# Packed attention with a gated feed-forward: pp @ w in groups of three f tiles, and where the attention's small products stand

## The chip, the cores and the metric

One core of one Trainium2 chip. The metric is the device time of one launch in microseconds (us); lower is better. Besides the times there is one profiled execution of the kernel, whose trace the rows below come from.

## What is computed

```python
def sm_attn(qq, kk, vv):
    s = scale * np.matmul(qq, kk.transpose(0, 1, 3, 2))
    ...                                  # softmax over the last axis -> a
    return np.matmul(a, vv)
p_packed = sm_attn(p, k, v)              # 8 batches, 8 heads, 32 packed rows
out = sm_attn(q, p_packed, p_packed)     # 576 rows a batch, 64 a head
...
x = out.transpose(0, 2, 1, 3).reshape(B * S, H * D)      # 4608 x 512
return ((x @ w_a) * (x @ w_b)) @ w_out   # w_a, w_b: 512 x 1536, w_out: 1536 x 512
```

All data are float32. The large products run as three products of parts (high by high, high by low, low by high), the small ones directly in float32.

## The kernel before

It works through eight batches. The second attention's last product and the two large products x @ w_a and x @ w_b are joined: out is a2 @ pp per head, so x @ w equals a2 times (pp @ w), and pp @ w (called g here) is small. For a batch, with the 1536 columns of w_a and w_b in twelve tiles of 128 (`ft` 0 to 11):

- **g** (`g_tiles`, matmuls on L332): eight products, of 64 rows by 32 columns each, for one pair of f tiles: four values of `r` by two of `e`, each with 512 moving columns (128 of w_a and 128 of w_b for both tiles). The four `r` stand on the four groups of 32 partitions of one PSUM bank, the two `e` in two banks of the pool `ps_x`. ACT casts each bank into `ghi` (L338), DVE subtracts for `glo` (L86).
- **mm1** (`mm1_half`, L351) for one f tile: 12 matmuls of 288 columns for w_a, then 12 for w_b, each half in a pair of banks of the pool `ps_m` ("m"), which has two such pairs that take turns. ACT copies the first half out (L363), DVE multiplies the second by it (L366), ACT casts the product to `h_hi` (L370), POOL makes `h_lo`.
- **mm2** (L377): after the twelve f tiles the batch's output tiles, each 36 matmuls of 512 columns; four or five such tiles a batch.

The order on each engine is written out by hand: instructions stand on their engine in the order in which the code calls them. Two things set it around the change. Pair c+1 of g is computed ahead of the odd tile `ft` = 2c+1 of the same batch; the first pair of the next batch is computed by the step `g` at the start of mm2. And the attention of the next batch is cut into steps, which the string `PLAN` deals out to numbered slots: `between` is called once after the first half and once after the second half of each mm1, and once after every three f tiles of mm2, so slots 2 ft and 2 ft + 1 belong to tile ft, and slots from 24 on to mm2. (`PLAN_0` does so for batch 0, which also has the weights to convert.) The steps that matter here:

- `S0`, `S1`: the first attention's scores for half e of the heads: 24 matmuls of 64 rows by 32 columns (each counts twice in a trace), L247, into the single pair of banks of the pool `ps_s` ("s").
- `r0`, `r1`, four times each: maximum and exponential; reciprocal; the transposes (L271 and L272, into "s"); the product with v (L281, 128 rows by 32 columns, into "s", then DVE L287 for `pp`).
- `T2 P0`: transposes of p and pp (L236). `s0`, `s1`: the second attention, begun by 16 recorded matmuls each on L297, e = 0 into "s" and e = 1 into "m"; DVE L302 then turns them.
- `q0`, `q1`, `k2`, `k3`: DVE turns a block of q or k (L119). `Lk`, `Lq`, `Lv`, `Lp`: SP issues loads.

In a trace each float32 matmul stands as two records, so a g of one pair is 16 records.

Of the kernel before, what the change touches and what calls it, by code (L numbers as in the profile page):

```python
# [9 lines left out]
F32R = mybir.dt.float32r  # L10
# [9 lines left out]
def tile_packed_attn_gated_ffn(  # L20
# [40 lines left out]
    ld = ep(tc.tile_pool(name="ld", bufs=1))  # L61
# [14 lines left out]
    w_ab = big.tile([P, NC, R, 4 * P], F32, name="w_ab")  # L76
# [154 lines left out]
    def turned(dst, src, back=0):  # L231

        tp = bank()
        cols = src.rearrange("p e d -> p (e d)")
        for i in range(2):
            nc.tensor.transpose(tp[:, P * i:P * i + P], cols[:, 64 * (i ^ back):64 * (i ^ back) + P], ident)  # L236
        nc.vector.tensor_copy(out=dst.rearrange("p i r j -> p (i r j)"), in_=tp[:, 0:2 * P])
# [84 lines left out]
        yield  # L322


    def g_tiles(b, c):

        assert len(to_do["C"]) <= len(pieces) - 4 * (c + 1)
        gps = [bank() for _ in range(E)]
        for r in range(R):
            for e in range(E):  # L330
                rows = slice(64 * e, 64 * e + 64)
                nc.tensor.matmul(  # L332
                    out=gps[e][J * r:J * r + J, :], lhsT=ppT[rows, 2 * (b % 2), r, :], rhs=w_ab[rows, c, r, :],
                    start=True, stop=True)
        ghi = ld.tile([P, E, 4 * P], F32R, name="ghi", bufs=2)
        glo = ld.tile([P, E, 4 * P], F32R, name="glo", bufs=2)
        for e in range(E):
            nc.scalar.copy(out=ghi[:, e], in_=gps[e])  # L338
            lo_part(glo[:, e], gps[e], ghi[:, e])
        gv = [t.rearrange("p e (a u f) -> p u e a f", a=2, u=2) for t in (ghi, glo)]  # L340
        return [(gv[0][:, u], gv[1][:, u]) for u in range(2)]


    def mm1_half(i, ghi, glo, ps=None, kts=range(E)):

        ps = bank_pair() if ps is None else ps
        steps = [(gt, at, kt) for kt in kts for gt, at in ((ghi, a2_hi), (ghi, a2_lo))]
        steps += [(glo, a2_hi, kt) for kt in kts]
        for n, (gt, at, kt) in enumerate(steps):
            for half in range(2):  # L350
                nc.tensor.matmul(  # L351
                    out=ps[:, half, 0:HS], lhsT=gt[:, kt, i, :], rhs=at[:, kt, HS * half:HS * half + HS],
                    start=(n == 0 and kt == 0), stop=(n == len(steps) - 1 and kt == E - 1))
        return ps

    def mm1(b, ft, ghi, glo, between):
        asb = sm.tile([P, 2, HS], F32, name="asb")
        if b == 0 and ft == 0:
            pa, pb = (mm1_half(i, ghi, glo, kts=(0,)) for i in range(2))
            mm1_half(0, ghi, glo, pa, (1,))  # L360
        else:
            pa, pb = mm1_half(0, ghi, glo), None
        nc.scalar.copy(out=asb, in_=pa[:, :, 0:HS])  # L363
        between()
        pb = mm1_half(1, ghi, glo, pb, (1,) if pb is not None else range(E))
        nc.vector.tensor_tensor(out=asb, in0=pb[:, :, 0:HS], in1=asb, op=ALU.mult)  # L366
        c0 = 64 * (b % 2)
        hh = h_hi[ft][:, c0:c0 + S]
        flat = asb.rearrange("p u t -> p (u t)")
        nc.scalar.copy(out=hh, in_=flat)  # L370
        lo_part(h_lo[ft][:, c0:c0 + S], flat, hh, nc.gpsimd)
        between()
# [43 lines left out]
    def drain(g):  # L416
        for _ in g:
            pass

    def emit(b, plan, tasks={}):  # L420

        for name in plan.split():
            if name in tasks:
                next(tasks[name], None)
                continue
            if name == "W":
                warm()
                continue
            if name in "ABCD":
                convert(name)  # L430
                continue
            what, e = name[:-1], int(name[-1])
            n = b + (e // 2 if b or what[0] == "L" else 0)
            if n >= B:
                continue
            if what == "S":
                if e == 0:
                    st[b] = [stage1(b, 0), stage1(b, 1), stage2(b, 0), stage2(b, 1)]
                next(st[b][e])
            elif what == "s":  # L440
                next(st[b][2 + e], None)
            elif what == "r":
                next(st[b][e], None)
            elif what == "T":
                turned(pT, p_nat.pop(n))
            elif what == "P":
                turned(ppT[:, b % 2:b % 2 + 2], pp.pop(b), b % 2)
            elif what in ("k", "q"):
                turn(what, n, e % 2) if b else turn_first(what, e)
            elif what == "Lk":  # L450
                load(k, "k", n, e % 2)
# [13 lines left out]
    TURN = ("0001110101")  # L465
    SUBS = ("0100")

    PLAN = (" | S0 | r0 |  | r0 | r0 |  | r0 Lv1 |  | S1 | r1 | q0 Lk2 | r1 |  |  | r1 q1 Lk3 |  | r1 Lv2 |  |  | "
            "T2 P0 |  |  | s0 s0 s1 g s0 |  | s1 | Lp4 s0 s1 s1 k2 | s0 | s0 | s1 s0 | s1 Lq2 | s1 | k3 Lq3")
    PLAN = dict(enumerate(PLAN.split("|")))  # L470
    PLAN_0 = ("A | C C | B A B A | B C C B C | A A | C | B | C B A T0 k0 Lp2 A | A A B B C Lq0 | C C k1 | A B A | "
# [5 lines left out]
    pieces = [(c, n) for c in range(NC) for n in range(4)] + [(NC, f) for f in range(NFT)]  # L477
    unloaded, to_do = list(pieces), {x: list(pieces) for x in "ABC"}
# [40 lines left out]
    def warm(n=9):  # L519

        x = bank_pair()[:, 0, :]
        t = firsts["k", 0].rearrange("p h t -> p (h t)")
        for _ in range(n):
            nc.tensor.matmul(out=x, lhsT=ident, rhs=t[:, 0:512], start=True, stop=True)

    def next_g(b):

        gnext[:] = g_tiles(b, 0)
        yield

    ET = mybir.EngineType
# [1 line left out]
    for name in FIRST.split():  # L533
        what, i = name[0], int(name[1])
# [5 lines left out]
            load_pieces(i)  # L540
        else:
            load_first(k if what == "k" else q, what, i)
    gnext = []
    tasks = {"g": next_g(0)}
    emit(0, START, tasks)
    drain(tasks["g"])
# [2 lines left out]
    for ft in range(NFT):  # L549
        h_hi.append(hp.tile([P, S + 64], F32R, name=f"h_hi{ft}"))  # L550
        h_lo.append(hp.tile([P, S + 64], F32R, name=f"h_lo{ft}"))

    for b in range(B):
        plan = dict(PLAN if b else PLAN_0)
        slot, tasks = [0], {"g": next_g(b + 1)}

        def between():
            emit(b + 1, plan.get(slot[0], "") if b + 1 < B else "", tasks)
            slot[0] += 1

        for ft in range(NFT):
            if ft % 2 == 0:
                gcur = list(gnext)
            elif ft + 1 < NFT:
                gnext[:] = g_tiles(b, ft // 2 + 1)
            mm1(b, ft, *gcur[ft % 2], between)
        tiles = [64 + P * i for i in range(4)] if b % 2 == 0 else [P * i for i in range(5)]
        last = tiles.pop() if b == B - 1 else None
        f0 = 0
        if b == 0:  # L570
            f0 = 9
            pairs = [bank_pair() for _ in range(2)]
            banks = [pairs[i % 2][:, i // 2, :] for i in range(4)]
            for f in range(f0):
                for i, c0 in enumerate(tiles):
                    mm2_part(banks[i], c0, [f])
                between()
            for _ in pieces:
# [50 lines left out]
```

## Time and profile before

| | us |
|---|---|
| median of 3 runs | 740.17 (739.3 to 740.57) |
| the profiled execution, its own time | 739.7 |
| its span, first to last instruction | 737.9 |
| TensorE (PE) busy | 724.8 |
| VectorE (DVE) busy | 302.4 |
| ScalarE (ACT) busy | 282.6 |
| GpSimd (POOL) busy | 212.5 |

The trace's views used below: the page's table of engines and its chain of waits by engine (which engine the end was waiting for, as shares of the span); the list of who waited for whom; the order of one engine's instructions in time, merged where alike; and busy times by stretch. A row of the order in time gives the start from the span's beginning in us, the time until its last record ends, engine, line, operation, output and inputs, shape, the count of records and, in brackets, how long the engine was idle before and for whom. Matmul records overlap, so the time that one takes from the next is the distance of their starts, not the length shown.

### The profile page before, as it was taken

Reading aid. Unit: us, or ns where it says so; the run is one execution under the profiler, and the core shown is the slowest. Engines: PE = TensorE matmul, PEld = TensorE weight load, DVE = VectorE, ACT = ScalarE, POOL = GpSimd, SP = SyncE. Lnnn points to the kernel's source line nnn. Section 1 sums busy time; section 2 is a strip of 40 time slices with the busy share of each in tenths; the row PEclk is TensorE's granted clock in tenths of the full one; section 3 lists DMA queues with packets and bytes.
Section 4 is the critical chain, followed back from the end, with each engine's and each line's share of the span. In section 5 each row is a group of like instructions: output and inputs, shape, how many; then the busy total and the mean of one; then the engine's idle time right before and its main releaser. Section 6 shows DMA issues by size and latency. Waiting matters only on the chain.

```text
span 737.9 us, 13756 instructions
## 1 busy us (share of the span) xinstructions
PE 724.8 (98%) x5862; PEld 606.0 (82%) x5862; DVE 302.4 (41%) x487; ACT 282.6 (38%) x495; POOL 212.5 (29%) x154
## 2 busy tenths in 40 slices
PE   6899999999999999999999999999999999999998
PEld 4488977888888888888888888888888888888887
DVE  2888655456114561344503545045610456023200
ACT  3788744553125531444204442144311543134300
POOL 0586752334003340234202341033400334023300
PEclk9999999999999999999999999999999999999999
DMA  8999945250501514033310333115050100000001
GB/s 251 379 260 297 257 88 99 57 97 17 97 30 33 98 30 84 16 66 70 74 48 16 65 71 77 47 33 97 5 104 30 34 1 17 28 15 2 1 29 43
DMA packets 171005, 58.30 MB, mean 79 GB/s; under 512 B 140608, under 2 KB 158784, under 8 KB 170944
## 3 DMA queue, kind: packets, MB, share of 16 engines
q1 hardware_dynamic: 170944, 57.43, 31.9%
q8 instruction: 46, 0.75, 0.4%
q14 instruction: 15, 0.12, 0.1%
HBM read 47.97 MB, written 9.44 MB: 78 GB/s over the span
## 4 chain that ended last, share of the span: by engine, by line
PE 95%; DVE 2%; DMA 1%; ACT 1%; issue 0%; SPq 0%; DVEq 0%; ACTq 0%
PE m L351 42%; PE m L377 40%; PE x L332 6%; PE s L281 2%; PE s L247 1%; PE s L271 1%; PE s L297 1%; DMA raw<-in_moe_w_b_dram 1%; DMA kn<-in_k_dram 1%; PE x L236 0%; DVE w_ab L200 0%; PE x L147 0%; PE m L297 0%; PE m L147 0%; SPq L177 0%
## 5 line engine op out<-in xcount | busy, mean ns | idle before, releaser
L377 PE MATMUL m<-wo,h_hi 128*128 128x512 f32 (+1 forms) x888 | 268.7, 385 | 0.0
L86 POOL TENSOR_TENSOR h_lo<-asb,h_hi 128x576 fp32r<-128x576 f32 x96 | 139.1, 1449 | 411.5 <-ACT h_hi L370 411.2
L377 PEld LDWEIGHTS m<-wo,h_hi 128*128 128x128 f32 x888 | 164.2, 188 | 39.0 <-DVE t L302 5.0
L366 DVE TENSOR_TENSOR asb<-m,asb 128x576 f32<-128x576 f32 x96 | 72.7, 757 | 281.9 <-PE m L351 278.6
L351 PE MATMUL m<-a_hi,ghi 128*128 128x288 f32 x768 | 170.7, 304 | 1.6 <-ACT ghi L338 1.5
L377 PE MATMUL m<-wo,h_lo 128*128 128x512 f32 (+1 forms) x444 | 170.4, 384 | 0.0
L351 PE MATMUL m<-a_lo,ghi 128*128 128x288 f32 x768 | 164.0, 295 | 0.3 <-DVE a_lo L86 0.3
L351 PEld LDWEIGHTS m<-a_hi,ghi 128*128 128x128 f32 x768 | 122.2, 188 | 37.5 <-issue 15.9
L351 PE MATMUL m<-a_hi,glo 128*128 128x288 f32 x768 | 133.5, 295 | 0.0
L351 PEld LDWEIGHTS m<-a_lo,ghi 128*128 128x128 f32 x768 | 123.5, 188 | 0.5 <-DVE a_lo L86 0.5
L370 ACT CAST h_hi<-asb 128x576 fp32r<-128x576 f32 x96 | 64.7, 674 | 143.6 <-DVE asb L366 143.5
L351 PEld LDWEIGHTS m<-a_hi,glo 128*128 128x128 f32 x768 | 112.8, 188 | 0.2 <-DVE glo L86 0.2
L377 PEld LDWEIGHTS m<-wo,h_lo 128*128 128x128 f32 x444 | 83.4, 188 | 16.6
L86 DVE TENSOR_TENSOR glo<-x,ghi 128x512 fp32r<-128x512 f32 x96 | 61.8, 686 | 53.3 <-ACT ghi L338 53.3
L363 ACT COPY asb<-m 128x576 f32<-128x576 f32 x96 | 61.6, 641 | 36.7 <-PE m L351 29.0
L412 ACT COPY asb<-m 128x512 f32<-128x512 f32 x24 | 14.1, 587 | 134.8 <-PE m L377 133.6
L332 PE MATMUL x<-w_ab,ppT 64*32 64x512 f32 x768 | 55.4, 597 | 0.2 <-DVE w_ab L200 0.2
L338 ACT CAST ghi<-x 128x512 fp32r<-128x512 f32 x96 | 51.4, 588 | 5.9 <-PE x L332 5.9
L119 DVE STREAM_TRANSPOSE xT<-nat 128x1152 f32<-128x1152 f32 x28 | 38.3, 1368 | 0.0
L412 ACT COPY wo_f<-m 128x512 f32<-128x512 f32 x11 | 6.5, 588 | 55.2 <-PE m L377 55.2
L315 POOL TENSOR_TENSOR t<-t,sum 128x576 f32<-128x576 f32 x14 | 16.5, 1178 | 25.0 <-DVE sum L314 25.0
L189 ACT ACTIVATE raw<-raw 128x512 f32<-128x512 f32 x36 | 23.1, 683 | 0.1
(108 smaller groups left out, 408.1 us busy)
## 6 DMA issues: line engine op xcount, KB each, us to landing
nat<-in_k_dram SPq DMA_DIRECT2D x56, 144.0 KB
nat<-in_q_dram SPq DMA_DIRECT2D x56, 144.0 KB
vt<-in_v_dram SPq DMA_DIRECT2D x28, 256.0 KB
raw<-in_moe_w_a_dram SPq DMA_DIRECT2D x12, 512.0 KB
raw<-in_moe_w_b_dram SPq DMA_DIRECT2D x12, 512.0 KB
raw<-in_moe_w_out_dram SPq DMA_DIRECT2D x12, 512.0 KB
out_dram<-asb SPq DMA_DIRECT2D x17, 256.0 KB
out_dram<-wo_f SPq DMA_DIRECT2D x10, 256.0 KB
```

What stands on the lines that cost most here:

```text
L86: return eng.tensor_tensor(out=dst, in0=src, in1=hi.bitcast(F32), op=ALU.subtract)
L119: nc.vector.transpose(out=xT.rearrange("p h t -> p (h t)"), in_=t.rearrange("p h x d -> p (h x d)"))
L189: nc.scalar.activation(out=high, in_=high, func=AF.Prelu, scale=2.0 ** -112, alpha=-2.0 ** 32)
L315: eng.tensor_tensor(out=s2, in0=s2, in1=sum2.unsqueeze(2).broadcast_to([P, TU, J]), op=ALU.mult)
L332: nc.tensor.matmul(out=gps[e][J * r:J * r + J, :], lhsT=ppT[rows, 2 * (b % 2), r, :], rhs=w_ab[rows, c, r, :], start=True, stop=True)
L338: nc.scalar.copy(out=ghi[:, e], in_=gps[e])
L351: nc.tensor.matmul(out=ps[:, half, 0:HS], lhsT=gt[:, kt, i, :], rhs=at[:, kt, HS * half:HS * half + HS], start=(n == 0 and kt == 0), stop= ...
L363: nc.scalar.copy(out=asb, in_=pa[:, :, 0:HS])
L366: nc.vector.tensor_tensor(out=asb, in0=pb[:, :, 0:HS], in1=asb, op=ALU.mult)
L370: nc.scalar.copy(out=hh, in_=flat)
L377: nc.tensor.matmul(out=o[:, cols], lhsT=ht[:, c0:c0 + P], rhs=wt[:, cols], start=(ft == 0 and n == 0), stop=(ft == NFT - 1 and n == 2))
L412: nc.scalar.copy(out=ob, in_=o)
```

## The change

In batches 1 to 7, g is computed for three f tiles at a time, four times a batch in place of six: ahead of tiles 2, 5 and 8, and at the step `g` in mm2. Each time one group has two tiles (512 columns, in two banks of `ps_x` as before) and one has a single tile (256 columns, the third). The third's two halves e stand in a pair of banks: the next of `ps_m` inside mm1 (issued ahead of the two-tile group), the pair of `ps_s` at the step in mm2 (issued behind it). `ghi` and `glo` become one tile each with four slots of an f tile; tile ft uses slot ft % 4. The number of columns is the same in all, as are the sizes in bytes of the casts and subtractions (128 x 512 for each). Batch 0 keeps its pairs. The columns of w are read in the order of f tiles, so the moving operand is read in runs of 128 columns.

`PLAN` is changed so that S0 stands in slot 3, and the product with v of r0 in slot 9, ahead of g; S1 comes in the same slot, behind g (a step after ";" is issued behind g). The product with v of r1 stands in slot 15, ahead of g. The transposes move from slots 5 and 15 to 7 and 13, `Lv1` from 7 to 9, `Lv2` from 17 to 15.

```diff
-    def g_tiles(b, c):
...
-        gps = [bank() for _ in range(E)]
-        for r in range(R):
-            for e in range(E):
-                rows = slice(64 * e, 64 * e + 64)
-                nc.tensor.matmul(
-                    out=gps[e][J * r:J * r + J, :], lhsT=ppT[rows, 2 * (b % 2), r, :], rhs=w_ab[rows, c, r, :],
-                    start=True, stop=True)
-        ghi = ld.tile([P, E, 4 * P], F32R, name="ghi", bufs=2)
-        glo = ld.tile([P, E, 4 * P], F32R, name="glo", bufs=2)
-        for e in range(E):
-            nc.scalar.copy(out=ghi[:, e], in_=gps[e])
-            lo_part(glo[:, e], gps[e], ghi[:, e])
...
+    ghi = ld.tile([P, E, 4, 2 * P], F32R, name="ghi")
+    glo = ld.tile([P, E, 4, 2 * P], F32R, name="glo")
+
+    def g_tiles(b, *groups, s=False):
+
+        for fts in groups:
+            c, i, n = fts[0] // 2, fts[0] % 4, len(fts)
...
+            if len(groups) > 1 and n == 1:
+                x = bank_pair(s)[:, :, 0:2 * P]
+                gps = [x[:, e, :] for e in range(E)]
+            else:
+                x, gps = None, [bank() for _ in range(E)]
+            for r in range(R):
+                for e in range(E):
+                    rows = slice(64 * e, 64 * e + 64)
+                    w = w_ab[rows, c, r, :].rearrange("p (a u f) -> p u a f", a=2, u=2)
+                    nc.tensor.matmul(
+                        out=gps[e][J * r:J * r + J, 0:2 * P * n], lhsT=ppT[rows, 2 * (b % 2), r, :],
+                        rhs=w if n == 2 else w[:, fts[0] % 2], start=True, stop=True)
+            parts = [(x, slice(0, E))] if x is not None else [(gps[e][:, 0:2 * P * n], e) for e in range(E)]
+            for part, e in parts:
+                hi, lo = (t[:, e, i] if n == 1 else t[:, e, i:i + 2].rearrange("p u c -> p (u c)") for t in (ghi, glo))
+                nc.scalar.copy(out=hi, in_=part)
+                lo_part(lo, part, hi)
...
-    PLAN = (" | S0 | r0 |  | r0 | r0 |  | r0 Lv1 |  | S1 | r1 | q0 Lk2 | r1 |  |  | r1 q1 Lk3 |  | r1 Lv2 |  |  | "
...
+    PLAN = (" |  |  | S0 | r0 | r0 |  | r0 |  | r0 Lv1 ; S1 | r1 | q0 Lk2 | r1 | r1 |  | r1 q1 Lk3 Lv2 |  |  |  | "
...
-        gnext[:] = g_tiles(b, 0)
+        g_tiles(b, *(((0, 1), (2,)) if b else ((0, 1),)), s=True)
...
+    G_AT = {2: ((3,), (4, 5)), 5: ((8,), (6, 7)), 8: ((9,), (10, 11))}
...
+            elif b and ft in G_AT:
+                g_tiles(b, *G_AT[ft])
+                emit(b + 1, late[0], tasks)
+            mm1(b, ft, between)
```

On TensorE, in a batch in the middle of the program. Before, the product with v of r0 (L281) stands by itself between two halves of mm1:

```order
L351 MATMUL m<-a_lo,ghi 128x288 x2
L351 MATMUL m<-a_hi,glo 128x288 x4
L281 MATMUL s<-vt,t_4232 32x64 x20
L351 MATMUL m<-a_hi,ghi 128x288 x2
L351 MATMUL m<-a_lo,ghi 128x288 x2
```

and one tile later the scores of S1 (L247) with a g of one pair (L332):

```order
L351 MATMUL m<-a_hi,glo 128x288 x4
L247 MATMUL s<-xT_3897,pT 32x288 x2
L247 MATMUL s<-xT_3985,pT 32x288 x2
L247 MATMUL s<-xT_3897,pT 32x256 x2
L247 MATMUL s<-xT_3985,pT 32x256 x2
L247 MATMUL s<-xT_3897,pT 32x32 x2
L247 MATMUL s<-xT_3985,pT 32x32 x2
L332 MATMUL x<-w_ab,ppT 32x512 x8
L351 MATMUL m<-a_hi,ghi 128x288 x2
```

Now, at the same place (lines have moved: g is L343, mm1 L361):

```order
L361 MATMUL m<-a_hi,glo 128x288 x4
L281 MATMUL s<-vt,t_4283 32x64 x20
L343 MATMUL m<-w_ab,ppT 32x256 x8
L343 MATMUL x<-w_ab,ppT 32x512 x8
L247 MATMUL s<-xT_3908,pT 32x288 x2
L247 MATMUL s<-xT_3996,pT 32x288 x2
L247 MATMUL s<-xT_3908,pT 32x256 x2
L247 MATMUL s<-xT_3996,pT 32x256 x2
L247 MATMUL s<-xT_3908,pT 32x32 x2
L247 MATMUL s<-xT_3996,pT 32x32 x2
L361 MATMUL m<-a_hi,ghi 128x288 x2
```

The product with v, a g of three tiles and the scores have moved into one stretch between two halves of mm1.

On TensorE at the start of mm2, the second attention (L297) and the next batch's first g, before and now:

```order
L297 MATMUL s<-xT_4414,ppT 32x288 x4
L297 MATMUL s<-xT_4510,ppT 32x288 x4
L297 MATMUL m<-xT_4414,ppT 32x288 x4
L297 MATMUL m<-xT_4510,ppT 32x288 x4
L332 MATMUL x<-w_ab,ppT 32x512 x8
L377 MATMUL m<-wo,h_hi_486 128x512 x2
```

```order
L297 MATMUL s<-xT_4427,ppT 32x288 x4
L297 MATMUL s<-xT_4529,ppT 32x288 x4
L297 MATMUL m<-xT_4427,ppT 32x288 x4
L297 MATMUL m<-xT_4529,ppT 32x288 x4
L343 MATMUL x<-w_ab,ppT 32x512 x8
L343 MATMUL s<-w_ab,ppT 32x256 x8
L387 MATMUL m<-wo,h_hi_486 128x512 x2
```

The third of that g has come in behind the pair and writes the pair of banks "s", which L297 wrote just before.

On DVE around the g of slot 15 (now) and of slot 17 (before): `pp` for r1 (L287), the turn of q1 (L119), the low parts of g (L86), the products of mm1 (L366, now L376):

```order
L119 STREAM_TRANSPOSE xT_5342<-nat_4859 128x1152
L366 TENSOR_TENSOR asb<-m,asb 128x576
L287 TENSOR_SCALAR pp<-s,rs 128x64
L86 TENSOR_TENSOR glo<-x,ghi 128x512 x2
L366 TENSOR_TENSOR asb<-m,asb 128x576
```

```order
L376 TENSOR_TENSOR asb<-m,asb 128x576 x2
L287 TENSOR_SCALAR pp<-s,rs 128x64
L119 STREAM_TRANSPOSE xT_4529<-nat_3998 128x1152
L86 TENSOR_TENSOR glo<-m,ghi 128x2x256
L86 TENSOR_TENSOR glo<-x,ghi 128x512 x2
L376 TENSOR_TENSOR asb<-m,asb 128x576 x2
```

The turn of q1 stood a tile ahead of the low parts and has moved to directly ahead of them; the first of them now reads the pair "m".

## Rows read from the trace of the kernel before

**Rows 1.** The page: engine TensorE (busy us, share, instructions), and the chain by engine.
```profile
PE 724.8 (98%) x5862; PEld 606.0 (82%) x5862; DVE 302.4 (41%) x487; ACT 282.6 (38%) x495; POOL 212.5 (29%) x154
...
PE 95%; DVE 2%; DMA 1%; ACT 1%; issue 0%; SPq 0%; DVEq 0%; ACTq 0%
```

**Rows 2.** Who waited: TensorE's longest (us in total, times, longest us).
```profile
PE x L236 <- DMA p_nat<-in_p_dram: 4.2, 1, 4.2
```

**Rows 3.** TensorE in time, batch 4: mm1 without a block, then g alone.
```profile
416.40 0.69 PE L351 MATMUL m<-a_hi,glo 128*128 128x288 f32 x4
...
417.21 0.42 PE L351 MATMUL m<-a_lo,ghi 128*128 128x288 f32 x2
...
418.00 0.69 PE L351 MATMUL m<-a_hi,glo 128*128 128x288 f32 x4
...
420.02 0.42 PE L351 MATMUL m<-a_lo,ghi 128*128 128x288 f32 x2
```

**Rows 4.** TensorE in time, batch 4: scores S1 with g.
```profile
409.72 0.69 PE L351 MATMUL m<-a_hi,glo 128*128 128x288 f32 x4
410.35 0.69 PE L247 MATMUL s<-xT,pT 64*32 64x288 f32 x20
...
412.43 0.42 PE L351 MATMUL m<-a_lo,ghi 128*128 128x288 f32 x2
```

**Rows 5.** TensorE in time, batch 4: transposes of r0 with g, then of r1 alone.
```profile
400.57 0.69 PE L351 MATMUL m<-a_hi,glo 128*128 128x288 f32 x4
...
403.12 0.42 PE L351 MATMUL m<-a_lo,ghi 128*128 128x288 f32 x2
...
422.40 0.70 PE L351 MATMUL m<-a_hi,glo 128*128 128x288 f32 x4
...
423.75 0.43 PE L351 MATMUL m<-a_lo,ghi 128*128 128x288 f32 x2
```

**Rows 6.** TensorE in time, batch 4: L281 of r0 alone, then of r1 with g.
```profile
405.51 0.69 PE L351 MATMUL m<-a_hi,glo 128*128 128x288 f32 x4
...
407.33 0.42 PE L351 MATMUL m<-a_lo,ghi 128*128 128x288 f32 x2
...
426.13 0.69 PE L351 MATMUL m<-a_hi,glo 128*128 128x288 f32 x4
...
428.81 0.43 PE L351 MATMUL m<-a_lo,ghi 128*128 128x288 f32 x2
```

**Rows 7.** TensorE in time: scores alone (batch 0); L297's second sixteen, then g.
```profile
58.89 0.69 PE L351 MATMUL m<-a_hi,glo 128*128 128x288 f32 x4
...
60.53 0.42 PE L351 MATMUL m<-a_lo,ghi 128*128 128x288 f32 x2
...
439.14 0.69 PE L297 MATMUL m<-xT,ppT 64*32 64x288 f32 x16
439.63 1.06 PE L332 MATMUL x<-w_ab,ppT 64*32 64x512 f32 x16
```

**Rows 8.** Batch 7 behind a g alone: TensorE, ACT and DVE in time.
```profile
653.57 0.42 PE L351 MATMUL m<-a_lo,ghi 128*128 128x288 f32 x2
...
654.88 0.43 PE L351 MATMUL m<-a_hi,ghi 128*128 128x288 f32 x2
...
653.72 1.07 ACT L338 CAST ghi<-x 128x512 fp32r<-128x512 f32 x2
...
654.33 1.29 DVE L86 TENSOR_TENSOR glo<-x,ghi 128x512 fp32r<-128x512 f32 x2 [1.23 <-ACT ghi L338]
```

**Rows 9.** DVE in time, batch 4; a stretch with its DMA share (last but one column).
```profile
416.63 1.37 DVE L119 STREAM_TRANSPOSE xT<-nat 128x1152 f32<-128x1152 f32 x1
...
427.73 0.28 DVE L287 TENSOR_SCALAR pp<-s,rs 128x64 f32<-128x64 f32 x1
...
439.49 0.77 DVE L302 STREAM_TRANSPOSE t<-s 128x576 f32<-128x576 f32 x1
...
414.00:418.00 4.00, 4.00 (x32) 4.00 (x31) 2.91 (x6) 2.68 (x5) 0.50 (x1) 1.00 0.01 2
```

More of the change, by code (lines that the diff above doesn't have):

```diff
@@ L322, in stage2 @@
         yield
-    def g_tiles(b, c):
-        assert len(to_do["C"]) <= len(pieces) - 4 * (c + 1)
-        gps = [bank() for _ in range(E)]
-        for r in range(R):
-            for e in range(E):
-                rows = slice(64 * e, 64 * e + 64)
-                nc.tensor.matmul(
-                    out=gps[e][J * r:J * r + J, :], lhsT=ppT[rows, 2 * (b % 2), r, :], rhs=w_ab[rows, c, r, :],
-                    start=True, stop=True)
-        ghi = ld.tile([P, E, 4 * P], F32R, name="ghi", bufs=2)
-        glo = ld.tile([P, E, 4 * P], F32R, name="glo", bufs=2)
-        for e in range(E):
-            nc.scalar.copy(out=ghi[:, e], in_=gps[e])
-            lo_part(glo[:, e], gps[e], ghi[:, e])
-        gv = [t.rearrange("p e (a u f) -> p u e a f", a=2, u=2) for t in (ghi, glo)]
-        return [(gv[0][:, u], gv[1][:, u]) for u in range(2)]
@@ L344, in mm1_half @@
-    def mm1_half(i, ghi, glo, ps=None, kts=range(E)):
+    ghi = ld.tile([P, E, 4, 2 * P], F32R, name="ghi")
[3 more added lines that the diff above has]
+            c, i, n = fts[0] // 2, fts[0] % 4, len(fts)
+            assert len(to_do["C"]) <= len(pieces) - 4 * (c + 1)
+            if len(groups) > 1 and n == 1:
[15 more added lines that the diff above has]
+                lo_part(lo, part, hi)
@@ L346, in mm1_half @@
+    def mm1_half(i, ft, ps=None, kts=range(E)):
         ps = bank_pair() if ps is None else ps
+        cols = slice(P * i, P * i + P)
         steps = [(gt, at, kt) for kt in kts for gt, at in ((ghi, a2_hi), (ghi, a2_lo))]
@@ L351, in mm1_half, with mm1 @@
                 nc.tensor.matmul(
-                    out=ps[:, half, 0:HS], lhsT=gt[:, kt, i, :], rhs=at[:, kt, HS * half:HS * half + HS],
+                    out=ps[:, half, 0:HS], lhsT=gt[:, kt, ft % 4, cols], rhs=at[:, kt, HS * half:HS * half + HS],
                     start=(n == 0 and kt == 0), stop=(n == len(steps) - 1 and kt == E - 1))
         return ps
-    def mm1(b, ft, ghi, glo, between):
+    def mm1(b, ft, between):
         asb = sm.tile([P, 2, HS], F32, name="asb")
         if b == 0 and ft == 0:
-            pa, pb = (mm1_half(i, ghi, glo, kts=(0,)) for i in range(2))
-            mm1_half(0, ghi, glo, pa, (1,))
+            pa, pb = (mm1_half(i, ft, kts=(0,)) for i in range(2))
+            mm1_half(0, ft, pa, (1,))
         else:
-            pa, pb = mm1_half(0, ghi, glo), None
+            pa, pb = mm1_half(0, ft), None
         nc.scalar.copy(out=asb, in_=pa[:, :, 0:HS])
         between()
-        pb = mm1_half(1, ghi, glo, pb, (1,) if pb is not None else range(E))
+        pb = mm1_half(1, ft, pb, (1,) if pb is not None else range(E))
         nc.vector.tensor_tensor(out=asb, in0=pb[:, :, 0:HS], in1=asb, op=ALU.mult)
@@ L466, in tile_packed_attn_gated_ffn @@
     SUBS = ("0100")
-    PLAN = (" | S0 | r0 |  | r0 | r0 |  | r0 Lv1 |  | S1 | r1 | q0 Lk2 | r1 |  |  | r1 q1 Lk3 |  | r1 Lv2 |  |  | "
-            "T2 P0 |  |  | s0 s0 s1 g s0 |  | s1 | Lp4 s0 s1 s1 k2 | s0 | s0 | s1 s0 | s1 Lq2 | s1 | k3 Lq3")
+    PLAN = (" |  |  | S0 | r0 | r0 |  | r0 |  | r0 Lv1 ; S1 | r1 | q0 Lk2 | r1 | r1 |  | r1 q1 Lk3 Lv2 |  |  |  | "
+            "| T2 P0 |  |  | s0 s0 s1 g s0 |  | s1 | Lp4 s0 s1 s1 k2 | s0 | s0 | s1 s0 | s1 Lq2 | s1 | k3 Lq3")
     PLAN = dict(enumerate(PLAN.split("|")))
@@ L542, in tile_packed_attn_gated_ffn @@
             load_first(k if what == "k" else q, what, i)
-    gnext = []
     tasks = {"g": next_g(0)}
@@ L551, in tile_packed_attn_gated_ffn @@
         h_lo.append(hp.tile([P, S + 64], F32R, name=f"h_lo{ft}"))
+    G_AT = {2: ((3,), (4, 5)), 5: ((8,), (6, 7)), 8: ((9,), (10, 11))}
     for b in range(B):
         plan = dict(PLAN if b else PLAN_0)
-        slot, tasks = [0], {"g": next_g(b + 1)}
+        slot, tasks, late = [0], {"g": next_g(b + 1)}, [""]
         def between():
-            emit(b + 1, plan.get(slot[0], "") if b + 1 < B else "", tasks)
+            steps, _, late[0] = (plan.get(slot[0], "") if b + 1 < B else "").partition(";")
+            emit(b + 1, steps, tasks)
             slot[0] += 1
         for ft in range(NFT):
[L562 to L566, printed above, removed]
+            if b == 0 and ft % 2 and ft + 1 < NFT:
+                g_tiles(b, (ft + 1, ft + 2))
+            elif b and ft in G_AT:
+                g_tiles(b, *G_AT[ft])
+                emit(b + 1, late[0], tasks)
+            mm1(b, ft, between)
         tiles = [64 + P * i for i in range(4)] if b % 2 == 0 else [P * i for i in range(5)]
```

## The prediction

> **What bounds the kernel now.** The page first: TensorE is busy for 724.8 of 737.9 us and the chain that ends last runs on it for 95% [rows 1]; no other engine passes 41%. The list of waits tells whether that busy time has holes: TensorE's longest wait is 4.2 us, once, for the first load [rows 2], and in the same list taken from 120 to 700 us it has no wait at all. So in batches 1 to 7 TensorE never stands still for anyone, and the time can only change by what TensorE does between the same large matmuls, or by a wait that the change makes. The granted clock is 1.00 in every stretch (the 2.4 GHz level), so it isn't the lever.
>
> What is to be had there is seen in TensorE's order in time. I call a stretch of small products between two halves of mm1 a block, and price it by distances of starts: from the last row of four mm1 matmuls ahead of it to the second row of mm1 behind it, less the 0.81 us (417.21 - 416.40) that the same six matmuls take without a block [rows 3]. Then:
> g alone 420.02 - 418.00 - 0.81 = 1.21 [rows 3]; scores with g 412.43 - 409.72 - 0.81 = 1.90 [rows 4]; transposes with g 1.74 and transposes alone 0.54 [rows 5]; the product with v alone 1.01, with g 1.87 [rows 6]; scores alone 0.83 [rows 7].
> The blocks of batches 1 to 7 repeat these within 0.02.
>
> How much of a block is work? Behind other small products, sixteen records of 288 columns take 0.49 us (439.63 - 439.14) [rows 7]. At that rate a g of 512 columns is 0.87 and one of 256 columns 0.44. So a block that holds g alone pays 1.21 - 0.87 = 0.34 for going into the small shape and back. Neighbours share that: v's product with g is 0.35 under the two apart (1.01 + 1.21 - 1.87). Not all do: transposes with g save 0.01 (0.54 + 1.21 - 1.74), since they enter the block almost free, and scores ahead of g save only 0.14 (0.83 + 1.21 - 1.90).
>
> **The change part by part.** Batches 1 to 6 before, without the block at mm2's start: S0 with g 1.90, transposes with g 1.74, v's product 1.01, S1 with g 1.90, g 1.21, transposes 0.54, v's product with g 1.87; sum 10.17.
> After: S0 with g and a third, 1.90 + d; transposes 0.54; v's product, g, third and S1, 1.87 + d + s; transposes 0.54; v's product, g and third 1.87 + d; and d more at mm2's start. Sum 6.72 + 4d + s. Here d is the third's group of sixteen records with 256 columns inside a block, and s the scores behind g.
>
> d: 0.44 by the rate above. As a check on a fixed cost for each record: L297's sixteen, 576 columns a tile in 0.49, and v's forty, 640 columns a tile in 0.66 (1.87 - 1.21), give together 0.0007 us a column and 5 ns a record, and with these d is 0.45. Less than 0.44 would mean streaming faster than any row. I take 0.44.
> s: between 0.49 (scores alone less the 0.34, and equal to L297's sixteen, which have the same 288 columns) and 0.69 (1.90 - 1.21, scores ahead of g). Ahead of g, the scores' pieces of 32 columns stand just in front of g's long matmuls on the same part of the array; behind g they end the block, and that end is already in the scores alone. So 0.49.
> Then a batch goes from 10.17 to 6.72 + 1.76 + 0.49 = 8.97: 1.20 less, 7.20 in six batches. Batch 7 has no attention beside it: five g alone, 6.05, become three with a third, 3 x (1.21 + 0.44) = 4.95: 1.10 less. Batch 0's step g, late in its mm2, pays one third more: 0.44. Together 7.20 + 1.10 - 0.44 = 7.86 us. The transposes cost the same wherever they stand. Casts, subtractions and columns are the same number and size, so ACT and DVE get no more work in sum, only three pieces in a row in place of two.
>
> **Waits that it adds.** (a) The third takes a turn in the pairs "m". The first half behind it then needs the other pair, which DVE's product of the tile before frees while g runs; the second half needs the pair of the third, which is free when DVE has made the third's low part. Tightest without attention, batch 7: the second half began at 654.88 [rows 8] and would come 0.44 later, 655.32. ACT's first cast starts at 653.72, held by its own queue and not by the product, so the third's takes its place; DVE's first low part starts at 654.33 and is done half of 1.29 later, 654.98. It is ready 0.34 early. In slot 15 the turn of q1, 1.37 us [rows 9], now stands ahead of the low parts on DVE: behind `pp`, which ends at 428.01 [rows 9], it ends at 429.38 and the third's low part at 430.03. The second half comes 654.88 - 653.57 = 1.31 behind the second row of mm1 [rows 8], so at 428.81 + 1.31 + 0.44 = 430.56 [rows 6]: 0.53 early. The low parts of the pair follow by 431.32 and are not needed before the next tile, 1.6 later. (b) At mm2's start the third writes "s" and waits for DVE's turn of it, which ends at 440.26 [rows 9]; the third is due at 439.63 + 0.87 = 440.50 [rows 7]. 0.24 early; if that cover were gone, mm2's first matmuls stand behind it, and each 0.1 would cost 0.6 in six batches. (c) S1 behind g needs "s" read by `pp`; g runs for 1.3 us between, `pp` takes 0.28 [rows 9]. (d) On SP's queue `Lv1` moves two slots back and its user two slots ahead. The load was issued behind v's product of r0, which is over by 407.33 [rows 6]; in the stretch 414 to 418 the DMA share is 0.01 [rows 9], so it is over within 7 us. From v's product to v's product there are now six halves of 1.6 and some 3 us of blocks, over 12 us. `Lv2` has half a batch; `Lk3` ahead of it waits as before. I price all four at nothing.
>
> **The rivals.** 1. A group costs more to enter than I think: a change of operands inside a block costs the 0.20 by which scores ahead of g exceed their stream (0.69 - 0.49). Then each of 28 thirds costs 0.20 more, 5.6, and the time is 737.9. For it: those rows. Against it: L297 to g and v to g show none. 2. Slower: the pair "m" comes free not with the third's low part but with the last of the three, or the third's is made last. By (a) the second half then waits until 431.32 in place of 430.56 in slot 15 (0.76), until 654.98 + 1.29 = 656.27 in place of 655.32 in batch 7 (0.95), and behind S0, which adds 0.69 of cover, 0.26: 6 x (0.76 + 0.26) + 3 x 0.95 = 9.0, so 741.3. It decides from a mean wait of 0.37 (7.86 / 21). Against it: the order shows the third's cast and low part first of three. 3. The moving operand is read in runs of 128 columns, which no row of before shows. There are 28 x 2 x 2 runs in thirds and 34 x 2 x 4 in pairs, 384; from 20 ns a run the gain is gone, and at 40 ns the time is 747.7. I take zero, as a run streams for 0.11 us, long enough to have the next address ready; nothing measured supports it. 4. The change doesn't do what it says, since it splits g into more matmuls: 28 x 16 = 448 records come in addition. At the most each costs 0.49 / 16 = 31 ns by itself on top of its columns (L297's sixteen taken as nothing but a fixed cost), 13.7 in sum, and the time is 746.0; from 17.5 ns each the gain is gone. Against it: those sixteen have more columns than a third and take 0.49 in all, so by this cause d could be 0.49 at most, 733.7.
> The Trainium skill speaks for that fourth case: "TensorEngine Tiling (Array Packing)", section Performance Considerations, Instruction Overhead, gives each matmul about 60 cycles. An estimate from that figure, 25 ns for each of the 448 records in series, is 11.2 us, and by it the time would be 743.5. The trace doesn't agree with the page for a cost in series: it would be 0.40 of the 0.49 us that L297's sixteen records take, columns included; parts of the array that work side by side can hide it.
>
> **How the numbers follow.** The sum against the profiled execution: span 737.9 - 7.9 = 730.0, its own time 739.7 - 7.9 = 731.8; the median of the runs is 0.5 above that execution: 740.17 - 7.86 = 732.3, the forecast, chance 0.80. Rival 1 (737.9) 0.08, rival 2 (741.3) 0.05, rival 3 0.04, rival 4 (746.0) 0.03. The forecast's own range: s at 0.69 adds 1.2 (733.5), d at 0.45 adds 0.3 (at 0.49, 1.4), and the waits under (a) and (b), none of them over 0.5 early, may turn into 0.1 each, some 2 us; runs differ by 0.6 to either side. That is 731.2 to 735.8, which holds 0.80. Runs of this kernel can tell 0.2% (1.5 us) from no change. Faster: the forecast and rival 1, 0.88. Within 0.2%: rival 2 or 3 at half their price, 0.04. Slower: 0.08.
>
> **What would show it.** Blocks: g with a third in batch 7 at 1.65; v's product, third, g, scores at 2.80; v's product, third, g at 2.31; S0's at 2.34. No wait of TensorE for DVE or ACT between 120 and 700 us. The busy times of ACT and DVE unchanged. I am wrong in the price if the blocks differ, and in the waits if TensorE's list shows `glo` or the turn of "s".

## The result and the profile after

| | before | changed |
|---|---|---|
| median of the runs, us | 740.27 (739.3 to 741.04, 5 runs) | 732.21 (731.64 to 733.02, 5 runs) |
| ratio to before | | 0.9891, 95% interval 0.9876 to 0.9905 |
| span of the profiled execution | 737.9 | 731.2 |

The forecast was 732.3. In the page of the changed kernel (busy us, share, instructions; then the chain by engine) TensorE is still the engine that sets the end. Its busy time is 7.6 us less than in [rows 1]. Its weight loads (PEld), which overlap its matmuls, are busy for 9.1 us more, with 224 records more; the busy time of the other engines is the same within 1 us:

```profile
PE 717.2 (98%) x6086; PEld 615.1 (84%) x6086; DVE 302.7 (41%) x487; ACT 281.7 (39%) x495; POOL 211.9 (29%) x154
...
PE 93%; DMA 3%; SPq 1%; ACT 1%; DVE 1%; issue 0%; DVEq 0%
```

TensorE's waits, first, second and last of seven (us, times, longest):

```profile
PE x L236 <- DMA p_nat<-in_p_dram: 4.3, 1, 4.3
PE x L147 <- DMA kn<-in_k_dram: 3.1, 1, 3.1
...
PE x L343 <- DVE w_ab L200: 0.2, 1, 0.2
```

All seven stand before 120 us; from 120 to 700 us there is none, as before. So no wait has taken the place of the blocks that went. The first loads land at different times: in this execution the first matmul of mm1 starts at 36.2 us against 35.1 in the trace of before, and over all the executions below between 34.6 and 36.4. That is why distances inside the program tell more than single spans here.

The cleanest such distance is from the first matmul of mm1 in batch 4 to that of batch 5. Before (TensorE in time):

```profile
389.63 0.42 PE L351 MATMUL m<-a_hi,ghi 128*128 128x288 f32 x2
...
473.41 0.42 PE L351 MATMUL m<-a_hi,ghi 128*128 128x288 f32 x2
```

Changed:

```profile
387.62 0.42 PE L361 MATMUL m<-a_hi,ghi 128*128 128x288 f32 x2
...
470.19 0.42 PE L361 MATMUL m<-a_hi,ghi 128*128 128x288 f32 x2
```

83.78 before, 82.57 now: 1.21 less. In the same way batches 1 to 6 save 1.16 to 1.21 each, 7.20 in sum, batch 7 to the end saves 1.09 (89.01 to 87.92), and batch 0 takes 0.49 more: 7.80 in all. Of these batch 0, in which the loads and the conversion of the weights still run, is no firm number: it takes 87.38 us here, and 87.19 to 88.43 in e1, e3, e4, e5, e7 and e8 below, which have the same order of instructions in it.

The blocks themselves, TensorE in time, batch 4 and then batch 7. They answer to [rows 3 to 6] and are priced in the same way (first row to last row of each, less 0.81):

```profile
393.48 0.69 PE L361 MATMUL m<-a_hi,glo 128*128 128x288 f32 x4
394.10 0.69 PE L247 MATMUL s<-xT,pT 64*32 64x288 f32 x20
...
396.61 0.42 PE L361 MATMUL m<-a_lo,ghi 128*128 128x288 f32 x2
...
405.93 0.69 PE L361 MATMUL m<-a_hi,glo 128*128 128x288 f32 x4
406.55 0.84 PE L281 MATMUL s<-vt,t 128*32 128x64 f32 x36
...
407.63 1.12 PE L343 MATMUL x<-w_ab,ppT 64*32 64x512 f32 x16
408.48 0.74 PE L247 MATMUL s<-xT,pT 64*32 64x256 f32 x24
...
409.53 0.42 PE L361 MATMUL m<-a_lo,ghi 128*128 128x288 f32 x2
...
418.86 0.69 PE L361 MATMUL m<-a_hi,glo 128*128 128x288 f32 x4
...
421.97 0.42 PE L361 MATMUL m<-a_lo,ghi 128*128 128x288 f32 x2
...
649.16 0.69 PE L361 MATMUL m<-a_hi,glo 128*128 128x288 f32 x4
649.78 0.66 PE L343 MATMUL m<-w_ab,ppT 64*32 64x256 f32 x16
650.24 1.06 PE L343 MATMUL x<-w_ab,ppT 64*32 64x512 f32 x16
...
651.61 0.42 PE L361 MATMUL m<-a_lo,ghi 128*128 128x288 f32 x2
```

| block | forecast | measured |
|---|---|---|
| scores S0, third, g | 2.34 | 2.32 |
| v's product, third, g, scores S1 | 2.80 | 2.79 |
| v's product, third, g | 2.31 | 2.30 |
| third and g alone (batch 7) | 1.65 | 1.64 |

The counts of these rows are records. S0 and S1 are 24 records each (20 and four shorter ones where g follows), which is 12 matmuls.

### The profile page after: what moved, and what is told of

Read it like the earlier page. It is cut to its first block, busy times and chain, and to the rows that moved or that the text cites. A ratio compares the mean times of both kernels' runs of the same rounds, so it can differ in the third digit from the quotient of the medians.

```text
span 731.2 us, 14205 instructions
## 1 busy us (share of the span) xinstructions
PE 717.2 (98%) x6086; PEld 615.1 (84%) x6086; DVE 302.7 (41%) x487; ACT 281.7 (39%) x495; POOL 211.9 (29%) x154
## 4 chain that ended last, share of the span: by engine, by line
PE 93%; DMA 3%; SPq 1%; ACT 1%; DVE 1%; issue 0%; DVEq 0%
PE m L361 42%; PE m L387 41%; PE x L343 4%; DMA raw<-in_moe_w_b_dram 2%; PE s L281 2%; PE m L343 1%; PE s L247 1%; DMA qn<-in_q_dram 1%; PE s L271 1%; PE s L297 1%; DVE w_ab L200 0%; PE x L236 0%; PE s L343 0%; PE m L297 0%; SPq L177 0%; SPq L169 0%
## 5 line engine op out<-in xcount | busy, mean ns | idle before, releaser
L86 POOL TENSOR_TENSOR h_lo<-asb,h_hi 128x576 fp32r<-128x576 f32 x96 | 138.1, 1439 | 399.9 <-ACT h_hi L380 399.6
L376 DVE TENSOR_TENSOR asb<-m,asb 128x576 f32<-128x576 f32 x96 | 72.7, 757 | 307.0 <-PE m L361 302.3
L361 PE MATMUL m<-a_hi,ghi 128*128 128x288 f32 x768 | 169.5, 302 | 1.6 <-ACT ghi L349 1.5
L361 PE MATMUL m<-a_lo,ghi 128*128 128x288 f32 x768 | 163.8, 295 | 0.3 <-DVE a_lo L86 0.3
L361 PEld LDWEIGHTS m<-a_hi,ghi 128*128 128x128 f32 x768 | 122.5, 188 | 20.7 <-issue 5.0
L361 PE MATMUL m<-a_hi,glo 128*128 128x288 f32 x768 | 133.7, 296 | 0.0
L361 PEld LDWEIGHTS m<-a_lo,ghi 128*128 128x128 f32 x768 | 123.9, 189 | 0.5 <-DVE a_lo L86 0.5
L361 PEld LDWEIGHTS m<-a_hi,glo 128*128 128x128 f32 x768 | 112.9, 188 | 0.2 <-DVE glo L86 0.2
L86 DVE TENSOR_TENSOR glo<-x,ghi 128x512 fp32r<-128x512 f32 x68 | 43.6, 682 | 4.5 <-ACT ghi L349 3.9
L343 PE MATMUL x<-w_ab,ppT 64*32 64x512 f32 x544 | 38.8, 591 | 0.2 <-DVE w_ab L200 0.2
L349 ACT CAST ghi<-x 128x512 fp32r<-128x512 f32 x68 | 36.6, 591 | 5.8 <-PE x L343 5.2
L119 DVE STREAM_TRANSPOSE xT<-nat 128x1152 f32<-128x1152 f32 x28 | 38.3, 1369 | 0.6 <-DMA nat<-in_k_dram 0.6
```

What stands on the lines that cost most here:

```text
L119: nc.vector.transpose(out=xT.rearrange("p h t -> p (h t)"), in_=t.rearrange("p h x d -> p (h x d)"))
L343: nc.tensor.matmul(out=gps[e][J * r:J * r + J, 0:2 * P * n], lhsT=ppT[rows, 2 * (b % 2), r, :], rhs=w if n == 2 else w[:, fts[0] % 2], sta ...
L349: nc.scalar.copy(out=hi, in_=part)
L361: nc.tensor.matmul(out=ps[:, half, 0:HS], lhsT=gt[:, kt, ft % 4, cols], rhs=at[:, kt, HS * half:HS * half + HS], start=(n == 0 and kt == 0 ...
```

## The experiments

Each starts from the changed kernel. "A batch" in the table is the distance from batch 4's first mm1 matmul to batch 5's, "batch 7" that from batch 7's to the end of the span. The runs were made in two sessions; the kernel before had medians of 740.03 (e1 to e4) and 740.52 (e5 to e8) in them.

| | median, us | ratio to before, 95% | a batch | batch 7 |
|---|---|---|---|---|
| before | 740.27 | | 83.78 | 89.01 |
| changed | 732.21 | 0.9891 (0.9876 to 0.9905) | 82.57 | 87.92 |
| e1 groups only | 738.62 | 0.9981 (0.9972 to 0.9991) | 83.61 | 87.93 |
| e2 places only | 737.30 | 0.9962 (0.9947 to 0.9977) | 83.31 | 89.01 |
| e3 third last | 743.93 | 1.0052 (1.0037 to 1.0067) | 84.13 | 91.07 |
| e4 S0 behind g | 731.63 | 0.9886 (0.9871 to 0.9900) | 82.37 | 87.92 |
| e5 third apart | 740.27 | 0.9995 (0.9986 to 1.0005) | 83.65 | 88.92 |
| e6 third split | 744.92 | 1.0056 (1.0040 to 1.0072) | 83.51 | 88.73 |
| e7 third in one run | 731.59 | 0.9885 (0.9867 to 0.9903) | 82.57 | 87.93 |
| e8 S0 behind g, not in batch 1 | 731.84 | 0.9880 (0.9864 to 0.9897) | 82.37 | 87.93 |

### e1 and e2: one half of the change at a time

e1 keeps the groups of three and takes the old plan:

```diff
-    PLAN = (" |  |  | S0 | r0 | r0 |  | r0 |  | r0 Lv1 ; S1 | r1 | q0 Lk2 | r1 | r1 |  | r1 q1 Lk3 Lv2 |  |  |  | "
+    PLAN = (" | S0 | r0 |  | r0 | r0 |  | r0 Lv1 |  | S1 | r1 | q0 Lk2 | r1 |  |  | r1 q1 Lk3 |  | r1 Lv2 |  |  | "
```

> g in groups of three as in the change, but PLAN as before (S0 in slot 1, v's product of r0 in slot 7 and of r1 in slot 17, S1 in slot 9 ahead of g). Theory, by blocks: S0 alone 0.83, g with a third 1.64, transposes 0.54, v's product alone 1.01, S1 with g and third 2.33, transposes with g and third 2.17, v's product alone 1.01, 0.43 at mm2: 9.96 a batch where before has 10.17. 1.3 less in six batches, 1.1 less in batch 7, 0.4 more in batch 0: 738.3. Rival (the grouping brings the gain, the places little): near the changed kernel, 732 to 734.

e2 keeps the pairs, six times a batch, and moves one product with v and S1:

```diff
-    G_AT = {2: ((3,), (4, 5)), 5: ((8,), (6, 7)), 8: ((9,), (10, 11))}
+    G_AT = {1: ((2, 3),), 3: ((4, 5),), 5: ((6, 7),), 7: ((8, 9),), 9: ((10, 11),)}
...
-        g_tiles(b, *(((0, 1), (2,)) if b else ((0, 1),)), s=True)
+        g_tiles(b, (0, 1), s=True)
...
-    PLAN = (" |  |  | S0 | r0 | r0 |  | r0 |  | r0 Lv1 ; S1 | r1 | q0 Lk2 | r1 | r1 |  | r1 q1 Lk3 Lv2 |  |  |  | "
+    PLAN = (" | S0 | r0 |  | r0 | r0 |  |  |  | r0 Lv1 ; S1 | r1 | q0 Lk2 | r1 |  |  | r1 q1 Lk3 |  | r1 Lv2 |  |  | "
```

> g in pairs, six times a batch as before, ahead of the same tiles; only v's product of r0 moves to slot 9, ahead of g, and S1 behind that g. Theory, by blocks: v's product with g and scores 1.87 + 0.49 in place of v's product alone 1.01 and scores with g 1.90: 0.55 less a batch, 3.3 in six, nothing in batches 0 and 7: 736.9. Rival (the places bring the gain): near 732. Rival (the two parts simply add): this and the run with groups alone together save 8, which the theory says they don't (4.6 to 5).

738.62 and 737.30, where 738.3 and 736.9 were expected. A batch saves 0.17 with the groups alone, 0.47 with the places alone, and 1.21 with both: the halves don't add, they need each other. Under the old plan the fewer g leave S0 and both of v's products standing by themselves, so the entries that g no longer pays are paid by its old neighbours. In batch 7, which has no neighbours, the groups alone bring the whole of it (87.93).

### e5: the third by itself

```diff
-    G_AT = {2: ((3,), (4, 5)), 5: ((8,), (6, 7)), 8: ((9,), (10, 11))}
+    G_AT = {1: ((3,),), 2: ((4, 5),), 5: ((6, 7),), 6: ((8,),), 7: ((9,),), 8: ((10, 11),)}
```

> The third group leaves its pair in mm1 and stands by itself, into the banks of ps_x: ahead of tile 1 (f tile 3), of tile 6 (8) and of tile 7 (9, behind the transposes). Same columns, same places of v's products and scores. Theory: each of the 21 thirds now pays its own way into the small shape and back, 0.34: 7.1 more, 739.3, with a lone third at 0.77 as a block. Rival (the gain is in reading w by f tiles or in the four slots, not in fewer blocks): 732.2.

740.27, where 739.3 was expected: the whole gain is gone. A batch is 1.08 longer than with the change, batch 7 by 1.00; three times 0.34 would be 1.02. In the profiled executions most of what lies above the expectation is in batch 0, where nothing was changed (88.37 against 87.38). A lone third and then a lone pair in batch 7, TensorE in time:

```profile
652.73 0.69 PE L361 MATMUL m<-a_hi,glo 128*128 128x288 f32 x4
653.35 0.66 PE L343 MATMUL x<-w_ab,ppT 64*32 64x256 f32 x16
...
654.31 0.42 PE L361 MATMUL m<-a_lo,ghi 128*128 128x288 f32 x2
...
656.69 0.69 PE L361 MATMUL m<-a_hi,glo 128*128 128x288 f32 x4
...
658.71 0.42 PE L361 MATMUL m<-a_lo,ghi 128*128 128x288 f32 x2
```

654.31 - 652.73 - 0.81 = 0.77 as expected, against the 0.43 that the same third adds beside its pair (1.64 - 1.21). The lone pair is 658.71 - 656.69 - 0.81 = 1.21, as in [rows 3]. What the change saves is the way in and out, not work: same columns, same slots, same order of reading, and no gain.

### e3: the third behind its pair

```diff
-    G_AT = {2: ((3,), (4, 5)), 5: ((8,), (6, 7)), 8: ((9,), (10, 11))}
+    G_AT = {2: ((4, 5), (3,)), 5: ((6, 7), (8,)), 8: ((10, 11), (9,))}
```

> The third stands behind the pair in mm1 (order of the two groups turned; same work, same blocks). Theory: the pair of banks m is then freed by the last of DVE's three low parts, and the second half of mm1 waits for it. From the changed kernel's trace that low part ends at 653.8 against 652.92 in batch 7 (0.9 late), 423.8 against 423.3 in slot 15 (0.5), 398.2 against 397.9 behind S0 (0.3), 410.8 against 410.9 in the block with S1 (0): 6 x 0.8 + 3 x 0.9 = 7.5 lost, 739.7, and TensorE's list of waits shows some 7 us for glo between 120 and 700 us. Rival (there is slack that I don't see, or the third's place doesn't matter): 732.2 and no wait.

743.93. The wait is there, and it is the pair of banks: TensorE's list from 120 to 700 us has one line, the 7.5 us that were expected (us, times, longest). TensorE, DVE and the weight loads in time show one of these waits in batch 7, and TensorE the one behind S0 in batch 4 (second fence):

```profile
PE m L361 <- DVE glo L86: 7.5, 15, 0.8
```

```profile
659.76 0.69 PE L361 MATMUL m<-a_hi,glo 128*128 128x288 f32 x4
661.24 0.53 PE L361 MATMUL m<-a_hi,ghi 128*128 128x288 f32 x2 [0.79 <-DVE glo L86]
661.61 0.42 PE L361 MATMUL m<-a_lo,ghi 128*128 128x288 f32 x2
...
660.51 0.68 DVE L86 TENSOR_TENSOR glo<-m,ghi 128x512 fp32r<-128x512 f32 x1
...
661.24 0.30 PEld L361 LDWEIGHTS m<-a_hi,ghi 128*128 128x128 f32 x2 [1.02 <-DVE glo L86]
...
400.23 0.69 PE L361 MATMUL m<-a_hi,glo 128*128 128x288 f32 x4
401.29 0.53 PE L361 MATMUL m<-a_hi,ghi 128*128 128x288 f32 x2 [0.36 <-DVE glo L86]
401.65 0.43 PE L361 MATMUL m<-a_lo,ghi 128*128 128x288 f32 x2
```

But the kernel loses 11.7 us against the changed one, not the 7.5 that were expected. The list counts TensorE's idle time from the modelled end of the last matmul. Four matmuls without a wait behind them take 0.53, so the half was due at 659.76 + 0.53 = 660.29. It started at 661.24, 0.95 late where the list has 0.79, and its second pair came 0.37 behind the first in place of 0.27: 1.05 in all. Its weights, too, were loaded only when the wait was over, at 661.24; those of a half that doesn't wait are loaded 0.13 ahead of it. So this wait costs 0.26 more than it is listed for, and the one behind S0 as much (401.65 - 400.23 - 0.81 = 0.61, listed 0.36); fifteen of them make 3.9, and 7.5 + 3.9 = 11.4. That the third stands first is worth 12 us, more than the whole change.

### e4 and e8: S0 behind its g

```diff
-    PLAN = (" |  |  | S0 | r0 | r0 |
+    PLAN = (" |  |  | ; S0 | r0 | r0 |
```

> S0 behind its g in place of ahead of it (one step behind a ;). Theory: scores behind g cost 0.49, ahead of it 0.69, so 0.20 less in six batches: 1.2, so 731.0, and the block at S0 falls from 2.33 to 2.12 in the trace. Rival (the cheap scores in slot 9 owe it to v's product in front and not to their place behind g): no change, 732.2.

The block, TensorE in time (its first, third and last row here), and the row of a wait in batch 1:

```profile
392.46 0.69 PE L361 MATMUL m<-a_hi,glo 128*128 128x288 f32 x4
...
394.39 0.70 PE L247 MATMUL s<-xT,pT 64*32 64x288 f32 x24
...
395.39 0.42 PE L361 MATMUL m<-a_lo,ghi 128*128 128x288 f32 x2
...
129.66 0.67 PE L343 MATMUL m<-w_ab,ppT 64*32 64x256 f32 x16 [0.59 <-ACT asb L373]
```

The block is 395.39 - 392.46 - 0.81 = 2.12, as expected, and a batch is 0.20 shorter. The rival falls: the scores are cheap because they stand behind g. But batch 1 now waits 0.59 for the pair "m": ACT's copy that frees it is late there, and S0 ahead of g had covered that wait. So the six batches bring 0.5 and not 1.2. e8 has the edit of e4 and leaves S0 ahead of g in batch 1 alone:

```diff
+        if b == 1:
+            plan[3] = "S0"
```

> S0 behind its g as in e4, but ahead of it in batch 1, where e4 shows TensorE waiting 0.6 for ACT's copy of the tile before (which waits for POOL's h_lo). Theory: no such wait, 0.20 less than the changed kernel in five batches, so 1.0 less: 731.2, and 90.53 us from batch to batch in place of 90.73. Rival (the wait comes back elsewhere): as e4, 731.6 or above.

No wait is left, batch 1 is back at the changed kernel's 90.73 us, the other five have 0.20 less each: 1.0 by the trace. The medians (731.84, 731.63, 732.21) can't tell the three apart; the intervals of the ratio overlap. e8 is the shortest by its distances, by an amount below what the runs can show.

### e6 and e7: how g is cut and read

```diff
+                    if n == 1:
+                        for a in range(2):
+                            nc.tensor.matmul(
+                                out=gps[e][J * r:J * r + J, P * a:P * a + P], lhsT=ppT[rows, 2 * (b % 2), r, :],
+                                rhs=w[:, fts[0] % 2, a], start=True, stop=True)
+                        continue
...
-                        rhs=w if n == 2 else w[:, fts[0] % 2], start=True, stop=True)
+                        rhs=w, start=True, stop=True)
```

> Each third's eight matmuls of 256 columns become sixteen of 128: 448 records more, same columns. Theory: a record's fixed cost is about 5 ns on one part of the array, eight parts side by side, so a third goes from 0.43 to 0.45: 0.02 x 28 = 0.6 more, 732.8. Rival (about 60 cycles for each matmul, in series, as in the Trainium skill, TensorEngine Tiling (Array Packing), Instruction Overhead): 448 x 25 ns = 11.2 more, 743.4.

744.92, and neither expectation holds. A block of batch 7, TensorE in time:

```profile
661.39 0.69 PE L367 MATMUL m<-a_hi,glo 128*128 128x288 f32 x4
662.01 0.71 PE L345 MATMUL m<-w_ab,ppT 64*32 64x128 f32 x32
662.48 1.32 PE L349 MATMUL x<-w_ab,ppT 64*32 64x512 f32 x16
664.09 0.42 PE L367 MATMUL m<-a_lo,ghi 128*128 128x288 f32 x2
```

The block is 1.89, 0.25 more than the changed kernel's 1.64. The third's own 32 records don't stretch: the pair begins 0.47 after them, where it began 0.46 after the sixteen of 256 columns. It is the pair behind that takes longer, 1.32 from its first start to its last end in place of 1.06; the starts of its first eight records are spread over 0.28 us, in the changed kernel over 0.05. So short matmuls have a price here, 0.25 / 16 = 16 ns for each added record, three times the 5 ns that I had worked out and less than the rival's 25 ns in series; it falls on what stands behind them. Why, was not tried. Scores ahead of g cost more than behind it too (e4), and they end in short pieces; that the cause is the same is not shown.

The blocks make 28 x 0.25 = 7.0 of the 12.7 us. Most of the rest is one event in batch 1, and it is no price of short matmuls. In three fences TensorE's line of waits, ACT in time, and the busy times by stretch (us; PE, weight loads, DVE, ACT, POOL; granted clock, DMA share, GB/s):

```profile
PE m L345 <- ACT asb L379: 3.1, 1, 3.1
```

```profile
134.02 0.64 ACT L379 COPY asb<-m 128x576 f32<-128x576 f32 x1 [4.71 <-DMA out_dram<-asb]
```

```profile
132.00:134.00 2.00, 0.00 (x0) 0.00 (x0) 0.00 (x0) 0.00 (x0) 0.00 (x0) 0.90 0.57 144
134.00:136.00 2.00, 1.28 (x40) 1.21 (x48) 0.76 (x1) 1.15 (x2) 0.00 (x0) 0.50 0.00 0
136.00:138.00 2.00, 2.00 (x17) 0.34 (x7) 0.69 (x1) 0.82 (x3) 1.41 (x1) 0.50 0.04 8
138.00:140.00 2.00, 2.00 (x9) 2.00 (x10) 1.56 (x3) 0.90 (x2) 0.00 (x0) 0.50 0.00 0
```

ACT's copy of the second tile waits for the store of batch 0's last output tile; the pair "m" stays taken, TensorE idles for 3.1 us, and in that idle time the granted clock falls to 0.50, the 1.2 GHz level, where it stays until about 140. Batch 1 is 97.46 us long in place of 90.73; 0.9 of that is its blocks, 5.8 this event. The mean granted clock was 0.995 to 0.997 in all four executions of e6, and 0.999 or 1.0 in all of the other kernels, so it was no single accident.

The store itself is not late. The same copy in the changed kernel (ACT in time), and that store as SP issues it, in the changed kernel and in e6:

```profile
130.05 0.64 ACT L373 COPY asb<-m 128x576 f32<-128x576 f32 x1 [1.54 <-POOL h_lo L86]
```

```profile
129.70 2.02 SPq L412 DMA_DIRECT2D out_dram<-asb  x4
```

```profile
130.72 1.92 SPq L418 DMA_DIRECT2D out_dram<-asb  x4
```

In the changed kernel the copy waits for POOL's `h_lo` of the tile before, and starts while the store is still being issued, so it can't be waiting for that; in the kernel before and in all the other runs, too, it doesn't wait for the store. In e6 the store is issued 1.0 us later, and ACT's first copy of the batch stands 0.8 later too (126.23 against 125.43). What differs is what the copy has to wait for. There are two buffers of `asb`, so in e6 this tile would stand in the one that the store reads; why the kernel came out so stays open.

```diff
-                        rhs=w if n == 2 else w[:, fts[0] % 2], start=True, stop=True)
+                        rhs=w if n == 2 else w_ab[rows, c, r, 0:2 * P], start=True, stop=True)
```

> The third reads the first 256 columns of the piece of w, in one run, in place of its own two runs of 128 (its results are then those of other columns). Theory: reading in runs costs nothing, 732.2, and the block of batch 7 stays at 1.64. Rival (a run has a price): 112 runs become 56; at 20 ns each 1.1 less, 731.1.

The block of batch 7, TensorE in time, first and last row:

```profile
647.60 0.70 PE L361 MATMUL m<-a_hi,glo 128*128 128x288 f32 x4
...
650.05 0.42 PE L361 MATMUL m<-a_lo,ghi 128*128 128x288 f32 x2
```

1.64, and the same 82.57 a batch: reading the third in two runs of 128 columns costs nothing that the trace can show. The pairs still read in four runs here, but e5's lone pair does so too, and its block is the 1.21 of before, where a pair is read in one run. Its profiled execution, 731.46 against 733.02, is shorter by what the first loads gave it (mm1 starts at 34.8 against 36.2) and by 0.18 in batch 0.

## Why the prediction held

**The bound** was right: TensorE without a hole from batch 1 on, so blocks are the only currency. **The sum** came out at 7.86 forecast and 7.80 in the trace. Its terms: 1.20 a batch forecast, 1.16 to 1.21 measured; 1.10 and 1.09 for batch 7; 0.44 and 0.49 for batch 0, where the agreement is chance, as batch 0 differs by 1.2 us between kernels that have it alike. **d** was 0.44, measured 0.43 (1.64 - 1.21), and 0.43 too at mm2's start in batch 4, where the stretch from the last four matmuls of mm1 to the second row of mm2 grows from 3.18 to 3.61. **s** was the choice that mattered among the bounds, 0.49 or 0.69. It is 0.49: 2.79 with S1 behind g, 2.30 without. e4 shows that the place behind g is what makes the scores cheap. The reason given, that their short pieces hurt what stands behind them, fits e6, where shorter thirds slow the pair behind; for the scores themselves it is not shown.

**The waits** were priced at nothing, rightly. The tightest, batch 7: DVE's low part of the third and the second half that needs its banks:

```profile
652.92 0.43 PE L361 MATMUL m<-a_hi,ghi 128*128 128x288 f32 x2
...
651.93 0.69 DVE L86 TENSOR_TENSOR glo<-m,ghi 128x512 fp32r<-128x512 f32 x1 [1.23 <-ACT ghi L349]
```

Done at 652.62, needed at 652.92: 0.30 early, 0.34 forecast. In slot 15 of batch 4 the turn of q1 ahead of it left 0.69 (422.60 against 423.29; 0.53 forecast), and at mm2's start "s" is free 0.23 early (436.62 against 436.85; 0.24 forecast). e3 shows that this margin is real and what stands behind it.

**The rivals.** Rival 1 (0.20 for each change of operands) falls with the measured d. Rival 2 is what e3 makes happen; its price, 9.0, was too small. It put 0.95 on a wait in batch 7, where e3 loses 1.05, but only 0.26 on the one behind S0, where e3 loses 0.61. Rival 3 falls with e7 for the thirds and with e5's lone pair for the pairs. Rival 4 counts 448 added records, which are those of the thirds; as fourteen pairs go, the program has 224 more (5862 and 6086 on the pages). It was rightly put aside for thirds of 256 columns, but the 5 ns for each record behind it were wrong as a general price: at 128 columns e6 shows 16. The two rows from which I solved for it hold a group of long matmuls and one of short ones, which don't obey one law.

**The span** of 731.2 against 730.0 forecast is the later start of mm1 in that execution, 1.1 us. That the median lies within 0.1 us of the forecast is luck in part: the forecast set it 0.5 above the profiled execution, as in the kernel before, and after the change it lies 0.8 below (732.21 and 733.02).

## What to carry to other kernels

When an engine has no idle time, price the changes of shape between its instructions: here the way into small products and back cost some 0.34 us for each block of g, of v's product or of scores (the transposes shared 0.01 of it with g), and cutting the number of blocks needed both fewer groups and neighbours placed beside them, neither of which brought much alone. Within a block, the scores with their short pieces cost 0.20 us less at its end than ahead of long matmuls. And where a buffer is lent out of a rotation, have the lent part read out first: the order of two groups was worth 12 us here.

## What the runs showed of the hardware

- A wait of TensorE costs more than the list says: 0.79 listed, 1.05 lost; the next weights are loaded only when it ends (e3).
- Groups of 128 columns slow the group behind them: 0.25 us for sixteen more records, with the short records themselves at full rate (e6).
- 3.1 us of idling in batch 1 cost 5.8: the granted clock fell while TensorE stood still and was at 0.50 from 134 to about 140 us (e6).
- The moving operand was read in runs of 128 columns at no cost that the trace shows: two runs for a third (1.64 either way, e7), four for a pair (1.21 either way, e5).
